# A key-value product with high and low halves side by side, and denominators in another order

## The chip, the cores and the metric

The kernel runs on one core of one Trainium2 chip. The core has five engines with an instruction stream each: TensorE (PE in the profile, with its weight loads shown apart as PEld), VectorE (DVE), ScalarE (ACT), GpSimd (POOL) and SyncE (SP, which here only issues DMAs). They meet through semaphores. The metric is the device time of one launch in microseconds, the median of several runs.

## The reference

The reference is one transformer block on a prompt of 2048 tokens of width 512, modulated by a condition vector. Cut to what matters here:

```
h = layernorm(x) * (1 + ca) + sa
q, k, v = split(h @ wqkv) into 32 heads of 16
pq, pk = phi(q), phi(k)          # phi(t) = (t + 1 if t > 0 else exp(t)) + 1e-6
kv  = sum over tokens of pk^T v  # a 16 x 16 block for each head
z   = sum over tokens of pk
o   = (pq kv) / (pq z + 1e-6)
x   = x + ga * (o @ wo)
...                              # then a second norm and a gated feed-forward block
```

All of it is float32.

## The kernel before, in words

The tokens are four chunks of 512, each chunk four tiles of 128 tokens, sixteen tiles in all; numbers 0 to 15 below are these. A matmul takes 128 x 128 weights and a moving operand of up to 512 columns. To keep float32 accuracy, each operand is split into a high part (a copy rounded to the format that TensorE takes, made by ScalarE) and a low part (the rest, a subtraction on VectorE), and a product is three matmuls: high by high, high by low, low by high. The function `product` (lines 215 to 221) issues these three for each of the four 128-row pieces of the contraction; `split` (lines 205 to 207) makes the two parts.

The kernel never forms the value vectors of all tokens. It sums over the tokens the product of the normed input and the key features, a 512 x 512 matrix T (in four PSUM banks, `tacc`), and gets the key-value blocks from T and the value weights afterwards. This is the small product of the change: `kv_part` (lines 789 to 796). For each of four pieces k of the contraction and each of four groups g of 128 output columns it issues the three matmuls with 128 moving columns: 48 in all, into one PSUM bank. Before it, `tt_high` (lines 780 to 784) adds the shift to a piece of T and has ScalarE copy out the high part, and `tt_low` (line 787) subtracts for the low part. After it, one VectorE multiplication (line 818) keeps the 16 x 16 blocks on the diagonal and clears the rest, and the result is split and multiplied by the output weights: `w_full` makes the folded weight of one group (product, then a multiplication by the gate at line 770), `w_split` its two parts.

The query features of a tile come from `proj` (a product), `q_a` (two ScalarE instructions, lines 327 and 328) and `q_b` (one on VectorE, line 331). The denominators are computed tile by tile: `den_p` multiplies the features by z (line 712, on POOL unless VectorE is named), `den_r` sums 16 neighbours (line 718, VectorE), `den_z` makes a constant that all tiles share (lines 706 and 707), `den_b` adds it and takes the reciprocal for a whole chunk at once (lines 727 and 728), `den_t` does the reduction, the addition and the reciprocal for single tiles (lines 734 to 736), and `den_c` divides the features (line 747). `den_q` is `den_p` on POOL for tiles by their running number.

The order of work is written out by hand: each engine runs its instructions in the order in which the program issues them, and a wait holds up what stands behind it on that engine. The part around the change stands in lines 774 to 835, and behind it come sixteen steps `y_step(i)`. In step i TensorE turns the features of tile i + 1 (`turn_a`, four transposes, line 846), which needs their division by `den_c(i + 1)`, and then forms the output of tile i (`y_a`, line 871), which needs the high part (ScalarE, line 850) and the low part (VectorE, line 854) of the turned tile i. In the lists of `after` stand further jobs: denominators, the sums of weight blocks of the feed-forward part (`right_sums`, four subtractions on POOL at line 1002) and their splits (`right_split`, low parts on POOL at line 1020).

SBUF tiles come from one pool of 99 buffers; PSUM has four banks for sums (`acc`) and four for products that are read at once (`bank`).

Of the kernel before, what the change touches and what calls it, by code (L numbers as in the profile page):

```python
# [9 lines left out]
F32R = mybir.dt.float32r  # L10
# [12 lines left out]
def tile_adaln_block(  # L23
# [41 lines left out]
    def f32(ap):  # L65
        return ap.bitcast(F32)
# [138 lines left out]
    def split(src, h, l, low=None):  # L205
        nc.scalar.activation(h, src, AF.Copy)  # L206
        (low or nc.vector).tensor_tensor(l, src, f32(h), op=ALU.subtract)  # L207
# [27 lines left out]
    def cut(pair, a, b):  # L235
        return pair[0][:, a:b], pair[1][:, a:b]
# [409 lines left out]
    for i in range(4, NT):  # L646
        ch, j = divmod(i, NJ)
        more = ch + 1 < NCH
        if i > 1:
            ahead[i + 2] = proj(i + 2, wk) if i + 2 < NT else proj(i + 6 - NT, wq)  # L650
        if i in q_at:
            qps = proj(q_at[i], wq)
        if i + 1 < NT:
            k_split_x(i + 1)
        if i + 1 < NT:
            k_split(i + 1)
        if more and j < 2:
            t_tile(i, 0, 1)
            nx.transpose(2 * j, 2 * j + 1)
            nx.modulated(ca, sa, 2 * j, 2 * j + 1, cast=nc.vector)  # L660
            norm[ch + 1:] = [nx]
        if ch + 2 < NCH and j == 1:
            nx2 = Norm(xts[ch + 2])
            nx2.stats(0, 1)
        if ch + 2 < NCH and j == 2:
            nx2.stats(2, 3)
            nx2.rstd_of()
        if ch + 2 < NCH and j == 3:
            nx = nx2
            nx.xhat(2)  # L670
        if i + 2 < NT:
            k_phi(i + 2, ahead.pop(i + 2))
        else:
            q_a(i + 6 - NT, ahead.pop(i + 2))
            q_b(i + 6 - NT)
        if i in q_at:
            q_a(q_at[i], qps)
            q_b(q_at[i])
        if i + 1 < NT:
            z_add(i + 1)  # L680
        if i + 1 == NT - 1:
# [12 lines left out]
        if i in extra:  # L694
            extra[i]()
    ga, gb, sb, cb = rows[2], rows[5], cols[3], cols[4]


# [5 lines left out]
    def den_z():  # L704

        nc.vector.reduce_sum(den0, zb.rearrange("p (h i) -> p h i", i=DH), axis=AX.X)
        nc.vector.tensor_scalar(den0, den0, EPS_PHI, EPS_DEN, op0=ALU.mult, op1=ALU.add)

    def den_p(ch, *js, on=None):
        for j in js:  # L710
            pzs[ch, j] = B("f")
            (on or nc.gpsimd).tensor_tensor(pzs[ch, j], phq[ch * NJ + j], zb, op=ALU.mult)  # L712

    def den_r(ch, *js):
        if ch not in dens:
            dens[ch] = T(small, "den", (P, NJ, NH))
        for j in js:
            nc.vector.reduce_sum(dens[ch][:, j], pzs.pop((ch, j)).rearrange("p (h i) -> p h i", i=DH), axis=AX.X)

    def den_a(ch, *js, on=None):  # L720

        for j in js:
            den_p(ch, j, on=on)
            den_r(ch, j)

    def den_b(ch):
        nc.vector.tensor_tensor(dens[ch], dens[ch], den0.unsqueeze(1).to_broadcast([P, NJ, NH]), op=ALU.add)
        nc.vector.reciprocal(dens[ch], dens[ch])

    def den_t(*tiles):  # L730
        for i in tiles:
            ch, j = divmod(i, NJ)
            den_r(ch, j)
            d = dens[ch][:, j]
            nc.vector.tensor_tensor(d, d, den0, op=ALU.add)
            nc.vector.reciprocal(d, d)

    def den_q(*tiles):
        for i in tiles:
# [31 lines left out]
            fs.append(f)  # L771
        return fs

    den_z()
    den_p(1, 0, 1)
    den_a(0, 0, 1, on=nc.vector)
    ps = proj(6, wq)
    fs, tt = [], []

    def tt_high(k):  # L780
        f = fs[k]
        nc.vector.scalar_tensor_tensor(f, zb, sa[:, k:k + 1], f, op0=ALU.mult, op1=ALU.add)
        tt.append((B("w", dt=F32R), B("w", dt=F32R)))
        nc.scalar.activation(tt[k][0], f, AF.Copy)

    def tt_low(k):
        nc.vector.tensor_tensor(tt[k][1], fs[k], f32(tt[k][0]), op=ALU.subtract)
# [20 lines left out]
    kvps = acc_bank()  # L808
# [7 lines left out]
    kvp = (B("xh", dt=F32R), B("xl", dt=F32R))  # L816
    kvf = B("n")
    nc.vector.tensor_tensor(kvf.rearrange("p (g c) -> p g c", g=KD), kvps.rearrange("p (g c) -> p g c", g=KD),
                            mask.unsqueeze(1).to_broadcast([P, KD, P]), op=ALU.mult)
    split(kvf, *kvp)  # L820
    q_a(8, ps)
    ps = proj(9, wq)
    q_b(8)
    den_b(0)
    q_a(9, ps)
    w_out(0, 1)
# [514 lines left out]
    y_step(4, q=12, after=[lambda: n2[0].rstd_of(3, 4, True), lambda: n2[0].xhat(0, 1, 2), lambda: den_t(8), lambda: den_q(10, 11)])  # L1341
    y_step(5, pre=[lambda: n2[0].xhat(3)], after=[lambda: den_t(9), lambda: den_q(12), lambda: right_sums(1)])
    y_step(6, pe=[lambda: ln2_turn(0, 0, 1)], after=[lambda: ln2_f(0, 0, 1), lambda: den_t(10), lambda: right_split(1)])
    for k in range(KH):
        lefts[k] = Left((0, 1), k).into(side)
    right_load(2)
    reload_x(12, 13, 14, 15)
    y_step(7, q=13, pe=[lambda: ln2_turn(0, 2, 3)], after=[lambda: n2[1].rstd_of(0, 3, True), lambda: ln2_f(0, 2, 3), lambda: den_t(11), lambda: L[0].split("a11")])
    y_step(8, after=[lambda: n2[1].rstd_of(3, 4, True), lambda: den_q(13), lambda: n2[1].xhat(0, 1, 2), lambda: den_t(12), lambda: L[1].split("a11")])
    y_step(9, q=14, pre=[lambda: n2[1].xhat(3)], pe=[lambda: ln2_turn(1, 0, 2)], mid=[lambda: ln2_f(1, 0, 2)],  # L1350
           after=[lambda: L[0].sum("s1"), lambda: den_t(13), lambda: L[0].split("a12"), lambda: L[0].sum("s3", on=nc.gpsimd)])
# [252 lines left out]
```

## Time and profile before

| | |
|---|---|
| time, median of 3 runs | 554.49 us (553.54 to 554.92) |
| span of the profiled execution | 552.4 us |
| TensorE busy | 545.8 us, 99% of the span |
| VectorE busy | 432.2 us, 78% |
| ScalarE busy | 299.5 us, 54% |
| GpSimd busy | 176.8 us, 32% |
| mean granted TensorE clock | 0.999 |

The page gives the span of the profiled execution, from its first to its last instruction; a run's time holds what lies around the span too. In a timeline, each row is one instruction or a run of equal ones: start, length, engine, line of the kernel, operation, output and inputs, shapes, count, and in brackets how long the engine stood idle before it and what ended that. A row of TensorE shows a matmul with its drain, so that rows overlap; what a matmul costs in a stream is the distance between starts. On VectorE, starts in a row of 512-column instructions are some 0.6 us apart, although each row is 0.68 long. A row that is longer than others of its shape has stood and waited in itself.

### The profile page before, as it was taken

The page shows a single profiled execution, that of the slowest core. Times are in us where ns is not written, and L with a number is a line of the kernel's source. Part 1 is how long each engine was busy: PE and PEld are TensorE (multiplying, and loading weights), DVE is VectorE, ACT ScalarE, POOL GpSimd, SP SyncE. Part 2 cuts the span into 40 slices and gives each one's busy share as a digit, 9 for nine tenths or more (in the row PEclk, how much of TensorE's full clock was granted, in tenths as well). Part 3 has the DMA queues.
Part 4 walks back from the last instruction along what each step waited for, and adds up shares of the span by engine and source line. Part 5 has one row for each costly group of instructions (what it writes and reads, how often), then busy time and mean ns, then how long its engine had stood idle before and what let it go on. Part 6 is the DMA issues. An engine that isn't in the chain of part 4 may idle for free. (4 is left out here: it accounts for less than half of the span.)

```text
span 552.4 us, 8146 instructions
## 1 busy us (share of the span) xinstructions
PE 545.8 (99%) x2775; PEld 460.1 (83%) x2775; DVE 432.2 (78%) x794; ACT 299.5 (54%) x535; POOL 176.8 (32%) x180
## 2 busy tenths in 40 slices
PE   8999999999999999999999999999999999999997
PEld 6888888888888888888888888878888888888886
DVE  6878779978998998865655767797577877879696
ACT  4876857456467876654545355463243534453540
POOL 2000000003527646353556644540002524242400
PEclk9999999999999999999999999999999999999999
DMA  8910224203230045195888634289786534342004
GB/s 256 373 57 1 76 77 152 77 0 77 78 115 2 0 154 189 39 316 180 285 286 274 222 123 163 87 312 391 231 259 218 173 131 138 129 146 86 1 0 153
DMA packets 58512, 83.24 MB, mean 151 GB/s; under 512 B 6564, under 2 KB 23720, under 8 KB 58472
## 3 DMA queue, kind: packets, MB, share of 16 engines
q1 hardware_dynamic: 56544, 81.16, 44.1%
q10 hardware_dynamic: 1928, 1.58, 0.9%
q8 instruction: 22, 0.36, 0.3%
q14 instruction: 18, 0.15, 0.1%
HBM read 53.02 MB, written 29.69 MB: 150 GB/s over the span
## 5 line engine op out<-in xcount | busy, mean ns | idle before, releaser
L1057 PE MATMUL bank<-h,w 128*128 128x512 f32 (+1 forms) x924 | 221.6, 391 | 0.2 <-POOL w L1020 0.2
L1057 PEld LDWEIGHTS bank<-h,w 128*128 128x128 f32 (+1 forms) x924 | 168.2, 186 | 36.2 <-POOL w L1020 0.6
L1063 ACT ACTIVATE bank<-bank 128x512 f32<-128x512 f32 (+2 forms) x46 | 26.2, 571 | 122.7 <-PE bank L1057 122.5
L1253 DVE TENSOR_TENSOR x<-acc,x 128x256 f32<-128x256 f32 x132 | 48.0, 414 | 13.7 <-PE acc L1226 13.1
L1226 PE MATMUL acc<-w,kh 128*128 128x256 f32 x308 | 57.1, 282 | 0.0
L1226 PEld LDWEIGHTS acc<-w,kh 128*128 128x128 f32 x308 | 50.6, 190 | 3.7
L1020 POOL TENSOR_TENSOR w<-raw,w 128x256 fp32r<-128x256 f32 (+3 forms) x22 | 24.7, 1121 | 73.7 <-ACT w L1013 64.1
L219 PE MATMUL bank<-w,h 128*128 128x512 f32 x112 | 44.1, 394 | 0.0
L221 PE MATMUL bank<-w,h 128*128 128x512 f32 x112 | 43.7, 390 | 0.0
L220 PE MATMUL bank<-w,h 128*128 128x512 f32 x112 | 43.6, 390 | 0.0
L1226 PE MATMUL acc<-w,kl 128*128 128x256 f32 x154 | 43.5, 283 | 0.0
L871 PE MATMUL acc<-w,xh 128*128 128x512 f32 x128 | 40.7, 399 | 0.0
L712 POOL TENSOR_TENSOR f<-h,zb 128x512 f32<-128x512 f32 x12 | 17.5, 1468 | 62.9 <-ACT zb L692 48.9
L262 POOL TENSOR_TENSOR rstd<-ve,half 128x4 f32<-128x4 f32 (+3 forms) x12 | 11.2, 935 | 81.4 <-DVE ve L259 68.0
L1083 DVE TENSOR_TENSOR phi<-bank,g 128x512 f32<-128x512 f32 (+1 forms) x22 | 15.1, 687 | 25.2 <-PE bank L1057 25.2
L1063 ACT ACTIVATE u<-bank 128x512 f32<-128x512 f32 (+1 forms) x44 | 26.1, 594 | 15.4 <-PE bank L1057 15.2
L1113 DVE TENSOR_TENSOR g<-bank,u 128x512 f32<-128x512 f32 (+1 forms) x22 | 15.2, 689 | 21.2 <-ACT u L1063 19.9
L1020 POOL TENSOR_TENSOR w<-t,w 128x512 fp32r<-128x512 f32 (+1 forms) x22 | 29.6, 1346 | 0.0
L1146 PE MATMUL acc<-w,kh 128*128 128x512 f32 (+1 forms) x76 | 29.6, 390 | 0.0
L1147 PE MATMUL acc<-w,kh 128*128 128x512 f32 (+1 forms) x76 | 29.6, 390 | 0.0
L1148 PE MATMUL acc<-w,kl 128*128 128x512 f32 (+1 forms) x76 | 29.6, 389 | 0.0
L277 ACT ACTIVATE n<-x,nmr,rstd 128x512 f32<-128x512 f32 x31 | 23.6, 808 | 10.9 <-DVE nmr L267 10.7
(204 smaller groups left out, 1187.0 us busy)
## 6 DMA issues: line engine op xcount, KB each, us to landing
right<-w SPq DMA_DIRECT2D x56, 256.0 KB, 3.7
w<-right SPq DMA_DIRECT2D x56, 256.0 KB, 4.3
x<-in_A_x_dram SPq DMA_DIRECT2D x22, 256.0 KB, 5.2
raw<-in_w_mod_dram SPq DMA_DIRECT2D x22, 256.0 KB, 3.7
raw<-in_B_w_down_dram SPq DMA_DIRECT2D x18, 256.0 KB, 3.0
side_s<-h SPq DMA_DIRECT2D x16, 256.0 KB, 2.6
h<-side_s SPq DMA_DIRECT2D x16, 256.0 KB, 5.3
raw<-in_A_wqkv_dram SPq DMA_DIRECT2D x12, 256.0 KB, 6.2
```

Source lines behind the costliest of these rows:

```text
L219: nc.tensor.matmul(ps, ah, bh, start=begin and i == 0, stop=False)
L220: nc.tensor.matmul(ps, ah, bl, start=False, stop=False)
L221: nc.tensor.matmul(ps, al, bh, start=False, stop=end and i == n - 1)
L871: nc.tensor.matmul(yps[i], x, y, start=fresh and k + n == 0, stop=k == KD - 1 and n == 2, skip_group_check=True)
L1020: sub = lambda out, x, y: (on or nc.gpsimd).tensor_tensor(out, x, f32(y), op=ALU.subtract)
L1057: mm = lambda x, y, **kw: nc.tensor.matmul(ps, x[:, k], y, skip_group_check=True, **kw)
L1063: nc.scalar.activation(out, x, AF.Copy)
L1146: nc.tensor.matmul(dn[j], hh[:n, a:b], dh[:n], start=i == 0, stop=False)
L1147: nc.tensor.matmul(dn[j], hh[:n, a:b], dl[:n], start=False, stop=False)
L1148: nc.tensor.matmul(dn[j], hl[:n, a:b], dh[:n], start=False, stop=i == n_of - 1)
L1226: mm = lambda x, y, **kw: nc.tensor.matmul(ps, x[:, a:b], y, skip_group_check=True, **kw)
L1253: nc.vector.tensor_tensor(xt[:, halves[at]], banks[b][m], xt[:, halves[at]], op=ALU.add)
```

## The change

Three things change.

First, the high and the low part of T lie side by side. For each piece k of the contraction and each half s of the columns there is a tile that holds, for each of two groups, 128 high and then 128 low columns. One matmul of 256 columns takes the high weights past both, and a second of 128 columns takes the low weights past the high columns: 32 matmuls in place of 48. The sums of high by low now stand apart, in the second 128 columns of each group, in two PSUM banks. They are copied to SBUF by ScalarE (`kv_side`) and added by two products with the identity (`kv_join`), which stand in the middle of the projection of tile 9. The mask is applied half by half (`kv_mask`). The identity is copied once into TensorE's format, in the key loop at tile 12. The splits of T become two instructions of 256 columns each in place of one of 512.

Second, of the multiplications of chunk 0 POOL takes tiles 2 and 3, and VectorE tiles 0 and 1, one of them ahead of the work on T and one behind it. The shared constant moves behind the query features of tiles 6 and 7. POOL takes tiles 6 and 4 after those features, and 8, 5 and 7 after the features of tile 8; before it had 4 and 5 first, then 6 and 7, and 8 in step 1.

Third, `den_t` takes two tiles in one addition and one reciprocal; the reductions stay single. Steps 0, 2, 4, 6 and 9 each handle a pair where single tiles were handled in almost every step.

```diff
@@ key loop
+        if i == NT - 4:
+            ident_r = B("w", (P, P), F32R)
+            nc.scalar.activation(ident_r, ident, AF.Copy)
@@ den_t
         for i in tiles:
-            ch, j = divmod(i, NJ)
-            den_r(ch, j)
-            d = dens[ch][:, j]
-            nc.vector.tensor_tensor(d, d, den0, op=ALU.add)
-            nc.vector.reciprocal(d, d)
+            den_r(*divmod(i, NJ))
+        (ch, a), n = divmod(tiles[0], NJ), len(tiles)
+        d = dens[ch][:, a:a + n]
+        nc.vector.tensor_tensor(d, d, den0.unsqueeze(1).to_broadcast([P, n, NH]), op=ALU.add)
+        nc.vector.reciprocal(d, d)
@@ around the small product
-    den_z()
-    den_p(1, 0, 1)
-    den_a(0, 0, 1, on=nc.vector)
+    den_p(0, 2, 3)
+    den_a(0, 0, on=nc.vector)
     ps = proj(6, wq)
...
-        tt.append((B("w", dt=F32R), B("w", dt=F32R)))
-        nc.scalar.activation(tt[k][0], f, AF.Copy)
+        tt.append([B("w", (P, KG, 2, P), F32R) for _ in range(2)])
+        for s in range(2):
+            nc.scalar.activation(tt[k][s][:, :, 0], pairs_of(f)[:, s], AF.Copy)
...
-        nc.vector.tensor_tensor(tt[k][1], fs[k], f32(tt[k][0]), op=ALU.subtract)
+        for s in range(2):
+            nc.vector.tensor_tensor(tt[k][s][:, :, 1], pairs_of(fs[k])[:, s], f32(tt[k][s])[:, :, 0], op=ALU.subtract)
...
-            for g in range(KD):
-                a, b = g * P, (g + 1) * P
-                (ah, al), (bh, bl) = cut(wv[k], a, b), cut(tt[k], a, b)
-                for n, (x, y) in enumerate(((ah, bh), (ah, bl), (al, bh))):
-                    nc.tensor.matmul(kvps[:, a:b], x, y, start=k + g + n == 0, stop=k == KD - 1 and n == 2,
+            for s in range(2):
+                for g in range(KG):
+                    a = (s * KG + g) * P
+                    (ah, al), both_b = cut(wv[k], a, a + P), tt[k][s][:, g]
+                    nc.tensor.matmul(kvps[s][:, g], ah, both_b, start=k + g == 0, stop=False, skip_group_check=True)
+                    nc.tensor.matmul(kvps[s][:, g, 0], al, both_b[:, 0], start=False, stop=k == KD - 1,
...
+    def kv_side(s):
+        kv_more.append(B("xh", (P, KG, P), F32R))
+        nc.scalar.activation(kv_more[s], kvps[s][:, :, 1], AF.Copy)
+    def kv_join(s):
+        nc.tensor.matmul(kvps[s][:, :, 0], ident_r, kv_more[s], start=False, stop=True, skip_group_check=True)
+    def kv_mask(s):
+        nc.vector.tensor_tensor(kvf[:, s], kvps[s][:, :, 0], mask.unsqueeze(1).to_broadcast([P, KG, P]), op=ALU.mult)
...
+    den_a(0, 1, on=nc.vector)
     q_a(6, ps)
...
-    den_p(1, 2)
+    den_p(1, 2, 0)
     ps = proj(8, wq)
-    den_a(0, 2, 3, on=nc.vector)
+    den_z()
+    den_r(0, 2, 3)
     kv_part(2, 3)
...
+    kv_side(0)
+    kv_side(1)
     q_a(8, ps)
-    ps = proj(9, wq)
+    ps = bank()
+    pairs = [(cut(norm[2].t[k], P, 2 * P), wq[k]) for k in range(KD)]
+    product(ps, pairs[:2], end=False)
+    kv_join(0)
+    kv_join(1)
+    product(ps, pairs[2:], begin=False)
+    kv_mask(0)
+    kv_mask(1)
+    split(kvf.rearrange("p s g c -> p (s g c)"), *kvp)
     q_b(8)
+    den_p(2, 0)
+    den_p(1, 1, 3)
     den_b(0)
@@ output steps
-    y_step(0, after=[lambda: q_b(11), lambda: den_q(7), lambda: den_t(4), lambda: right_sums(0)])
-    y_step(1, after=[lambda: den_t(5), lambda: den_q(8)])
-    y_step(2, after=[lambda: den_t(6), lambda: den_q(9), lambda: right_split(0)])
-    y_step(3, after=[lambda: den_t(7), lambda: n2[0].rstd_of(0, 3, True)])
+    y_step(0, after=[lambda: q_b(11), lambda: den_t(4, 5), lambda: right_sums(0)])
+    y_step(1, after=[lambda: den_q(9)])
+    y_step(2, after=[lambda: den_t(6, 7), lambda: right_split(0)])
+    y_step(3, after=[lambda: n2[0].rstd_of(0, 3, True)])
...
```

The steps from 4 on change in the same way: pairs (8, 9), (10, 11) and (12, 13) in steps 4, 6 and 9; tiles 14 and 15 stay single.

More of the change, by code (lines that the diff above doesn't have):

```diff
@@ L772, in w_full, with pairs_of @@
         return fs
-    den_z()
-    den_p(1, 0, 1)
-    den_a(0, 0, 1, on=nc.vector)
+    den_p(0, 2, 3)
+    den_a(0, 0, on=nc.vector)
     ps = proj(6, wq)
     fs, tt = [], []
+    KG = KD // 2
+    def pairs_of(x):
+        return x.rearrange("p (s g c) -> p s g c", s=2, g=KG)
     def tt_high(k):
@@ L782, in tt_high @@
         nc.vector.scalar_tensor_tensor(f, zb, sa[:, k:k + 1], f, op0=ALU.mult, op1=ALU.add)
-        tt.append((B("w", dt=F32R), B("w", dt=F32R)))
-        nc.scalar.activation(tt[k][0], f, AF.Copy)
+        tt.append([B("w", (P, KG, 2, P), F32R) for _ in range(2)])
+        for s in range(2):
+            nc.scalar.activation(tt[k][s][:, :, 0], pairs_of(f)[:, s], AF.Copy)
     def tt_low(k):
-        nc.vector.tensor_tensor(tt[k][1], fs[k], f32(tt[k][0]), op=ALU.subtract)
+        for s in range(2):
+            nc.vector.tensor_tensor(tt[k][s][:, :, 1], pairs_of(fs[k])[:, s], f32(tt[k][s])[:, :, 0], op=ALU.subtract)
     def kv_part(*ks):
         for k in ks:
-            for g in range(KD):
-                a, b = g * P, (g + 1) * P
-                (ah, al), (bh, bl) = cut(wv[k], a, b), cut(tt[k], a, b)
-                for n, (x, y) in enumerate(((ah, bh), (ah, bl), (al, bh))):
-                    nc.tensor.matmul(kvps[:, a:b], x, y, start=k + g + n == 0, stop=k == KD - 1 and n == 2,
-                                     skip_group_check=True)
+            for s in range(2):
[4 more added lines that the diff above has]
+                    nc.tensor.matmul(kvps[s][:, g, 0], al, both_b[:, 0], start=False, stop=k == KD - 1,
+                                     skip_group_check=True)
+    kv_more = []
+    def kv_side(s):
[3 more added lines that the diff above has]
+        nc.tensor.matmul(kvps[s][:, :, 0], ident_r, kv_more[s], start=False, stop=True, skip_group_check=True)
+    kvf = B("n", (P, 2, KG, P))
+    kvp = (B("xh", (P, D), F32R), B("xl", (P, D), F32R))
+    def kv_mask(s):
+        nc.vector.tensor_tensor(kvf[:, s], kvps[s][:, :, 0], mask.unsqueeze(1).to_broadcast([P, KG, P]), op=ALU.mult)
     for k in range(KD):
@@ L805, in tile_adaln_block @@
     tt_low(KD - 1)
+    den_a(0, 1, on=nc.vector)
     q_a(6, ps)
     q_tile(7)
-    kvps = acc_bank()
+    kvps = [T(ps_acc, "acc", (P, KG, 2, P)) for _ in range(2)]
     kv_part(0, 1)
@@ L811, in tile_adaln_block @@
     q_b(7)
-    den_p(1, 2)
+    den_p(1, 2, 0)
     ps = proj(8, wq)
-    den_a(0, 2, 3, on=nc.vector)
+    den_z()
+    den_r(0, 2, 3)
     kv_part(2, 3)
[L816 to L820, printed above, removed]
-    q_a(8, ps)
-    ps = proj(9, wq)
+    kv_side(0)
+    kv_side(1)
+    q_a(8, ps)
+    ps = bank()
[7 more added lines that the diff above has]
+    split(kvf.rearrange("p s g c -> p (s g c)"), *kvp)
     q_b(8)
+    den_p(2, 0)
+    den_p(1, 1, 3)
     den_b(0)
@@ L1335, in tile_adaln_block @@
     right_load(1)
-    y_step(0, after=[lambda: q_b(11), lambda: den_q(7), lambda: den_t(4), lambda: right_sums(0)])
-    y_step(1, after=[lambda: den_t(5), lambda: den_q(8)])
-    y_step(2, after=[lambda: den_t(6), lambda: den_q(9), lambda: right_split(0)])
-    y_step(3, after=[lambda: den_t(7), lambda: n2[0].rstd_of(0, 3, True)])
+    y_step(0, after=[lambda: q_b(11), lambda: den_t(4, 5), lambda: right_sums(0)])
+    y_step(1, after=[lambda: den_q(9)])
+    y_step(2, after=[lambda: den_t(6, 7), lambda: right_split(0)])
+    y_step(3, after=[lambda: n2[0].rstd_of(0, 3, True)])
     reload_x(8, 9, 10, 11)
-    y_step(4, q=12, after=[lambda: n2[0].rstd_of(3, 4, True), lambda: n2[0].xhat(0, 1, 2), lambda: den_t(8), lambda: den_q(10, 11)])
-    y_step(5, pre=[lambda: n2[0].xhat(3)], after=[lambda: den_t(9), lambda: den_q(12), lambda: right_sums(1)])
-    y_step(6, pe=[lambda: ln2_turn(0, 0, 1)], after=[lambda: ln2_f(0, 0, 1), lambda: den_t(10), lambda: right_split(1)])
+    y_step(4, q=12, after=[lambda: n2[0].rstd_of(3, 4, True), lambda: n2[0].xhat(0, 1, 2), lambda: den_t(8, 9), lambda: den_q(10, 11)])
+    y_step(5, pre=[lambda: n2[0].xhat(3)], after=[lambda: den_q(12), lambda: right_sums(1)])
+    y_step(6, pe=[lambda: ln2_turn(0, 0, 1)], after=[lambda: ln2_f(0, 0, 1), lambda: den_t(10, 11), lambda: right_split(1)])
     for k in range(KH):
@@ L1347, in tile_adaln_block @@
     reload_x(12, 13, 14, 15)
-    y_step(7, q=13, pe=[lambda: ln2_turn(0, 2, 3)], after=[lambda: n2[1].rstd_of(0, 3, True), lambda: ln2_f(0, 2, 3), lambda: den_t(11), lambda: L[0].split("a11")])
-    y_step(8, after=[lambda: n2[1].rstd_of(3, 4, True), lambda: den_q(13), lambda: n2[1].xhat(0, 1, 2), lambda: den_t(12), lambda: L[1].split("a11")])
+    y_step(7, q=13, pe=[lambda: ln2_turn(0, 2, 3)], after=[lambda: n2[1].rstd_of(0, 3, True), lambda: ln2_f(0, 2, 3), lambda: L[0].split("a11")])
+    y_step(8, after=[lambda: n2[1].rstd_of(3, 4, True), lambda: den_q(13), lambda: n2[1].xhat(0, 1, 2), lambda: L[1].split("a11")])
     y_step(9, q=14, pre=[lambda: n2[1].xhat(3)], pe=[lambda: ln2_turn(1, 0, 2)], mid=[lambda: ln2_f(1, 0, 2)],
-           after=[lambda: L[0].sum("s1"), lambda: den_t(13), lambda: L[0].split("a12"), lambda: L[0].sum("s3", on=nc.gpsimd)])
+           after=[lambda: L[0].sum("s1"), lambda: den_t(12, 13), lambda: L[0].split("a12"), lambda: L[0].sum("s3", on=nc.gpsimd)])
     y_step(10, pe=[lambda: ln2_turn(1, 1, 3)], mid=[lambda: ln2_f(1, 1, 3)],
```

## The prediction

> **What bounds the kernel now.** I read the page's busy shares first, then TensorE's own waits (between 120 and 340 us that answer is empty), then the table by stretches and the timelines of the engines around the edit. The shares, and three stretches (in each row the columns are the stretch, its length, and the busy time of PE, PEld, DVE, ACT and POOL with instruction counts, then PE clock and DMA):
>
> ```profile
> span 552.4 us, 8146 instructions
> ## 1 busy us (share of the span) xinstructions
> PE 545.8 (99%) x2775; PEld 460.1 (83%) x2775; DVE 432.2 (78%) x794; ACT 299.5 (54%) x535; POOL 176.8 (32%) x180
> ```
> ```profile
> 132.94:135.57 2.63, 2.63 (x26) 2.63 (x24) 2.53 (x5) 1.90 (x4) 0.00 (x0) 1.00 0.80 201
> 138.40:141.03 2.63, 2.63 (x26) 2.63 (x24) 2.56 (x4) 0.00 (x0) 2.63 (x2) 1.00 0.00 0
> 143.00:156.00 13.00, 13.00 (x63) 10.62 (x62) 12.52 (x21) 8.76 (x16) 3.19 (x3) 1.00 0.22 70
> ```
>
> TensorE is never idle here, so each microsecond taken from it is worth one, and each wait put in front of it costs one. The third row holds the danger: behind the small product DVE works 12.52 of 13.00 us. It is no bound there, but it has 0.48 us to spare, while POOL works only 3.19 us. TensorE's timeline behind the small product, the dates that the other engines must meet:
>
> ```profile
> 143.86 0.39 PE L219 MATMUL bank<-w,xh 128*128 128x512 f32 x1
> ...
> 150.67 0.60 PE L846 MATMUL bank<-ident,h 128*128 128x128 f32 x4
> ...
> 152.97 0.73 PE L871 MATMUL acc<-w,xh 128*128 128x512 f32 x2
> 153.53 0.40 PE L871 MATMUL acc<-w,xl 128*128 128x512 f32 x1
> ...
> 159.06 0.60 PE L846 MATMUL bank<-ident,h 128*128 128x128 f32 x4
> ```
>
> 143.86 is the first use of the masked product, 150.67 the turn of query tile 0, 152.97 the first output product and 153.53 its third matmul (the first that needs a low part), 159.06 the turn of tile 3.
>
> **The change, part by part.** *The product on TensorE.* Each half of it, 24 matmuls of 128 columns, took 2.63 us: 0.110 each. A half now has 8 of 256 columns and 8 of 128. For 256 columns with new weights each time, the chain of work has:
>
> ```profile
> 412.66 1.43 PE acc L1226 x12
> ```
>
> That is 0.119 each, so a half costs 8 x 0.119 + 8 x 0.110 = 1.83 and saves 0.80; both save 1.60. The two identity products have 256 columns: 0.24. Net -1.36. Bounds: a wide matmul costs no less than a narrow one (net -1.51) and no more than two narrow ones (net +0.24). I take 0.119, the same shape. A rule bears on this: the Trainium skill, "TensorE: Matmul & The Clock Gate", section Back-to-back issue gap, gives some 81 ns for each 128-column matmul that brings its own weights. By that figure the 16 matmuls saved would be worth 1.3 us instead of 1.75, and the whole forecast would rise by about 0.45 (an estimate from that page). The trace's 110 ns does not agree and decides.
>
> *The splits of T.* Four ACT copies and four DVE subtractions become eight each, of half the width. Before, the last two subtractions were:
>
> ```profile
> 134.15 1.47 DVE L787 TENSOR_TENSOR w<-n,w 128x512 fp32r<-128x512 f32 x2
> 141.95 0.63 ACT L206 ACTIVATE xh<-n 128x512 fp32r<-128x512 f32 x1 [4.75 <-DVE n L818]
> L1253 DVE TENSOR_TENSOR x<-acc,x x132: 405/414/425, 370.7 to 541.2; 128x256 f32<-128x256 f32 x132
> ```
>
> They ended at 135.62. The second half of the product now starts at 138.40 - 0.80 = 137.60, so 2 us cover them, and DVE also starts on T earlier, as the shared denominator and one of its two early tiles move behind it. I price the split at nothing; without the cover it would be four times 2 x 0.41 - 0.68, 0.6 us. The copy of the identity is one small ACT instruction long before its use: nothing. DVE loses two multiplications of chunk 0 to POOL and gets one back later; by 141.2 its queue is empty enough for the mask.
>
> *The join.* The second half ends at 141.03 - 1.60 = 139.43. Two ACT copies must be done when the six matmuls put between (half of 143.86 - 141.03, 1.42) are through, at 140.85. The first bank closes four matmuls early, so even at the 0.63 of a full-width copy they end near 140.4. The joins end at 141.1. Two masks of 0.41 (the L1253 row) follow, started a little apart: 141.95. The high copy, 0.63: 142.6. The low part, 0.68 with POOL out of the way: 143.35. TensorE has finished the other six matmuls at 142.5, waits 0.2 for the high part, and 0.25 before its third matmul for the low. Of 1.36 some 0.9 is left: it leaves this place 0.9 early.
>
> *The denominators.* Here I expect the gain to go. DVE and POOL as they were:
>
> ```profile
> 142.62 1.19 DVE L207 TENSOR_TENSOR xl<-n,xh 128x512 fp32r<-128x512 f32 x1 [0.70 <-ACT xh L206]
> 143.77 0.69 DVE L331 SCALAR_TENSOR_TENSOR h<-bank,h 128x512 f32<-128x512 f32 x1
> ...
> 146.89 1.29 DVE L207 TENSOR_TENSOR w<-n,w 128x512 fp32r<-128x512 f32 x2
> 148.10 0.68 DVE L331 SCALAR_TENSOR_TENSOR h<-bank,h 128x512 f32<-128x512 f32 x1
> 148.70 0.68 DVE L747 SCALAR_TENSOR_TENSOR h<-h,den 128x512 f32<-128x512 f32 x1
> 149.30 1.28 DVE L770 TENSOR_TENSOR n<-bank,row 128x512 f32<-128x512 f32 x2
> 150.50 0.68 DVE L747 SCALAR_TENSOR_TENSOR h<-h,den 128x512 f32<-128x512 f32 x1
> 151.10 0.68 DVE L207 TENSOR_TENSOR w<-n,w 128x512 fp32r<-128x512 f32 x1
> 151.94 0.69 DVE L854 TENSOR_TENSOR xl<-bank,xh 128x512 fp32r<-128x512 f32 x1 [0.15 <-ACT xh L850]
> 152.54 0.68 DVE L207 TENSOR_TENSOR w<-n,w 128x512 fp32r<-128x512 f32 x1
> ...
> 155.82 0.68 DVE L718 TENSOR_REDUCE den<-f 128x32 f32<-128x512 f32 x1
> 156.53 0.19 DVE L735 TENSOR_TENSOR den<-den,den 128x32 f32<-128x32 f32 x1
> 156.75 0.35 DVE L736 RECIPROCAL den<-den 128x32 f32<-128x32 f32 x1
> 157.02 0.63 DVE L747 SCALAR_TENSOR_TENSOR h<-h,den 128x512 f32<-128x512 f32 x1
> ```
> ```profile
> 142.52 0.74 POOL L1002 TENSOR_TENSOR t<-raw,t 128x256 f32<-128x256 f32 x1
> 144.60 1.31 POOL L712 TENSOR_TENSOR f<-h,zb 128x512 f32<-128x512 f32 x1 [1.34 <-PE bank L220]
> 148.93 1.62 POOL L712 TENSOR_TENSOR f<-h,zb 128x512 f32<-128x512 f32 x1 [3.02 <-DVE h L331]
> ```
>
> A DVE instruction that reads two SBUF tiles and a POOL instruction do not run together: the subtraction at 142.62 took 1.19 for its usual 0.68, until POOL's instruction of 142.52 had ended and 0.55 more. Where both have a queue they take turns:
>
> ```profile
> 217.46 0.74 POOL L1002 TENSOR_TENSOR t<-raw,t 128x256 f32<-128x256 f32 x1
> 218.16 1.19 POOL L1002 TENSOR_TENSOR t<-raw,raw 128x256 f32<-128x256 f32 x1
> ```
> ```profile
> 217.53 2.36 DVE L207 TENSOR_TENSOR h<-s,h 128x512 fp32r<-128x512 f32 x2
> ```
>
> Two subtractions took 2.36 there and 1.29 at 146.89. The Trainium skill, "SBUF — State Buffer", section Who interferes with whom, calls it an exclusive lock for a whole instruction and exempts DVE instructions with one SBUF input; if the four of those in this stretch waited too, 0.5 us each as at 142.62, my sum would rise by 2 us (an estimate).
>
> POOL's order is now: tiles 2 and 3 of chunk 0, then 6 and 4, then 8, 5 and 7, then the four weight sums of the first right block (0.74 each, before done by 143.26), then 9. Tile 8 needs the query feature that DVE finishes behind the mask and the split, at about 144.0, so POOL stands idle until then and after it works without a pause: three multiplications of some 1.25, four sums, one more multiplication, 8 us of work from 144.15, where 2.9 us stood. On DVE it meets six two-tile instructions. DVE arrives 0.5 early (no 1.19 this time). Asked, granted, ended:
> - low of output weight 0: asked 146.39, POOL's second multiplication ends 146.63, done 147.2 (before 147.57).
> - low of weight 1: behind POOL's third, 148.45; done 149.0 (before 148.18).
> - division of query tile 0: asked 149.54, behind the first sum; done 150.3 (before 149.38).
> - division of tile 1: asked 151.43, behind the third; done 152.3 (before 151.18).
> - low of weight 2: behind the fourth sum; done 153.6 (before 151.78). Then the low of the turned tile 0, which waits for nobody: 154.25 (before 152.63).
> - low of weight 3: behind the multiplication of tile 9; done 155.4 (before 153.22).
>
> 3.5 us of waits. The pair of denominators adds a reduction (0.71 with its gap) and some 0.2 of reciprocal ahead of the division of tile 3: 160.5 where it was 157.65. The pairs save six additions and the start of six reciprocals later, some 1.5 us of DVE, on which TensorE does not wait.
>
> Against TensorE's dates: tile 0 turns at 150.36 (wanted 149.8 with the 0.9 in hand; before 150.67). The third matmul of the first output product waits for 154.25 plus a signal: 154.3, against 153.53, +0.77. The turn of tile 3 waits for the division at 160.5: 160.56, against 159.06, +1.5. Behind it DVE has caught up: its next pair comes only after two steps, and tile 5's turn lies behind a whole query projection. Each of the six waits is good to 0.3; bounds of their sum are 0 (POOL always loses) and 6 us (each meets a POOL instruction at its start). I take +1.4.
>
> **The sum.** The profiled execution spans 552.4, the median is 554.49, so 2.1 lies around the span and stays. 552.4 + 1.4 + 2.1 = 555.9.
>
> **Rivals.** *Slower by more.* The first of the six waits has a margin of 0.24: if POOL's second multiplication ends before 146.39 instead of at 146.63, the low of weight 0 waits for the whole third one, the low of weight 1 then ends at 149.5, and 0.5 more is carried to tile 3: 556.4 and, where the sums fall badly too, up to 557.4. For it: the margin is smaller than my error. Against: POOL's start at 144.15 follows DVE's own work, so both shift together. Chance 0.30.
> *The gain stays.* DVE had finished the division of tile 0 at 149.38 for a turn at 150.67, 1.3 early; if POOL gives way more often than the rows at 217 show, that slack covers the lateness: 554.49 - 0.9 = 553.6. Chance 0.20.
> *No gain at all.* The 256 columns cost as much as two narrow matmuls: the product saves nothing, everything behind comes 1.6 later: 557.5. Against: the L1226 row. Chance 0.04.
> The forecast has 0.46.
>
> **How the numbers follow.** About 0.3%, 1.66 us, is what a measurement of this kernel can tell from no change. The gain rival reaches 552.8 with a quarter of its chance: faster 0.05. The forecast lies within, with 0.06 of its 0.46 beyond 556.15: same 0.40 + 0.15 = 0.55; slower 0.06 + 0.30 + 0.04 = 0.40. The range runs from a little under the gain rival, 553.4, to the bad end of the slower one, 557.4.
>
> **What would show it.** Right: the small product at 0.114 per matmul; POOL unbroken from 144 to 155; lows at L207 and divisions at L747 of 1.2 to 1.9 us there; PE waits named after DVE at the first output product and the turn of tile 3. Wrong: those lows at 0.68, PE without a gap until 170, or POOL done with the sums before 144.

## The result, and the profile after

The kernel after takes 557.05 us (median of 5 runs, 556.37 to 557.51), the kernel before 554.49 us (5 runs, 553.54 to 555.01): a ratio of 1.0044, 95% interval 1.0032 to 1.0056. It is slower by 2.56 us. The profiled execution spans 555.0 us where 552.4 stood. From the page (busy us of each engine, its share of the span, its instructions), and the table by stretches with the two halves of the small product and the 13 us behind it (columns as in the prediction):

```profile
span 555.0 us, 8120 instructions
PE 545.8 (98%) x2761; PEld 458.8 (83%) x2761; DVE 428.3 (77%) x787; ACT 300.5 (54%) x542; POOL 180.6 (33%) x182
```
```profile
132.80:134.59 1.79, 1.79 (x17) 1.79 (x16) 1.79 (x6) 1.18 (x4) 0.00 (x0) 1.00 0.24 60
137.40:139.19 1.79, 1.79 (x17) 1.79 (x16) 1.75 (x4) 0.26 (x1) 1.79 (x2) 1.00 0.85 239
143.00:156.00 13.00, 12.11 (x56) 9.40 (x56) 12.86 (x19) 7.51 (x14) 10.10 (x8) 1.00 0.19 65
```

Each half of the product went from 2.63 to 1.79 us. In the third row POOL went from 3.19 to 10.10 us, and TensorE, which had no gap there, stands still for 0.89 us. VectorE has fewer instructions in that row (19 for 21) and is busier: the longer ones stand and wait inside themselves. TensorE's own waits between 120 and 340 us (what it waited for, then us in total, times, longest), where the answer of before was empty:

```profile
PE bank L881 <- DVE h L750: 1.4, 2, 1.2
PE bank L219 <- DVE h L331: 0.9, 1, 0.9
```

The answer counts from the end of a matmul's row, drain included (148.04 + 0.39 to 149.32 is 0.89). So it shows a stop shorter than it is in the stream of starts, and leaves short ones out: 142.42 stands 0.40 behind 142.02 instead of the usual 0.23. TensorE's timeline around these waits:

```profile
142.02 0.40 PE L221 MATMUL bank<-w,h 128*128 128x512 f32 x1
142.42 0.50 PE L219 MATMUL bank<-w,xh 128*128 128x512 f32 x1
142.76 0.40 PE L220 MATMUL bank<-w,xh 128*128 128x512 f32 x1
143.15 0.50 PE L221 MATMUL bank<-w,xl 128*128 128x512 f32 x1
143.49 0.39 PE L219 MATMUL bank<-w,xh 128*128 128x512 f32 x1
...
148.04 0.39 PE L221 MATMUL bank<-w,xl 128*128 128x512 f32 x1
149.32 0.50 PE L219 MATMUL bank<-w,h 128*128 128x512 f32 x1 [0.89 <-DVE h L331]
...
150.82 0.60 PE L881 MATMUL bank<-ident,h 128*128 128x128 f32 x4
...
153.69 0.40 PE L906 MATMUL acc<-w,xl 128*128 128x512 f32 x1
...
159.60 0.66 PE L881 MATMUL bank<-ident,h 128*128 128x128 f32 x4 [0.26 <-DVE h L750]
...
174.98 0.39 PE L906 MATMUL acc<-w,xl 128*128 128x512 f32 x1
176.55 0.63 PE L881 MATMUL bank<-ident,h 128*128 128x128 f32 x4 [1.19 <-DVE h L750]
```

Against the same places of before, TensorE uses the masked product at 142.42 (before 143.86, -1.44), turns tile 0 at 150.82 (150.67, +0.15), reaches the third matmul of the first output product at 153.69 (153.53, +0.16), turns tile 3 at 159.60 (159.06, +0.54) and tile 7 at 176.55 (174.72, +1.83). The last turn, of tile 15, stays +1.82 late (239.69 for 237.87) and TensorE's last matmul +1.85 (550.08 for 548.23). Of the 1.44, 0.14 was there before the product began (132.80 for 132.94). So three places make the loss: the wait at 149.32, which eats the whole gain of the product (from 1.03 early at 148.04 to 0.15 late), tile 3, which adds some 0.4, and tile 7, which adds 1.2. VectorE's and POOL's timelines of after at these places:

```profile
146.13 2.54 DVE L207 TENSOR_TENSOR w<-n,w 128x512 fp32r<-128x512 f32 x2
148.59 0.68 DVE L331 SCALAR_TENSOR_TENSOR h<-bank,h 128x512 f32<-128x512 f32 x1
149.19 0.68 DVE L750 SCALAR_TENSOR_TENSOR h<-h,den 128x512 f32<-128x512 f32 x1
149.79 1.28 DVE L773 TENSOR_TENSOR n<-bank,row 128x512 f32<-128x512 f32 x2
150.99 0.73 DVE L750 SCALAR_TENSOR_TENSOR h<-h,den 128x512 f32<-128x512 f32 x1
151.63 1.22 DVE L207 TENSOR_TENSOR w<-n,w 128x512 fp32r<-128x512 f32 x1
...
153.38 1.19 DVE L207 TENSOR_TENSOR w<-n,w 128x512 fp32r<-128x512 f32 x1
...
158.92 0.63 DVE L750 SCALAR_TENSOR_TENSOR h<-h,den 128x512 f32<-128x512 f32 x1
...
172.44 1.27 DVE L721 TENSOR_REDUCE den<-f 128x32 f32<-128x512 f32 x2
173.74 0.95 DVE L738 TENSOR_TENSOR den<-den,den 128x64 f32<-128x64 f32 x1
174.73 0.55 DVE L739 RECIPROCAL den<-den 128x64 f32<-128x64 f32 x1
175.20 1.21 DVE L750 SCALAR_TENSOR_TENSOR h<-h,den 128x512 f32<-128x512 f32 x1
```
```profile
143.84 4.27 POOL L715 TENSOR_TENSOR f<-h,zb 128x512 f32<-128x512 f32 x3 [4.37 <-DVE h L331]
148.08 1.17 POOL L1037 TENSOR_TENSOR t<-raw 128x256 f32<-128x256 f32 x1
149.32 1.14 POOL L1037 TENSOR_TENSOR t<-raw,t 128x256 f32<-128x256 f32 x1
...
152.27 1.75 POOL L715 TENSOR_TENSOR f<-h,zb 128x512 f32<-128x512 f32 x1
...
173.31 4.24 POOL L715 TENSOR_TENSOR f<-h,zb 128x512 f32<-128x512 f32 x3
```

*At 149.32.* The first product of the projection of tile 11 needs a PSUM bank, and that bank holds the projection of tile 9 until `q_b(9)`, the L331 row at 148.59, has read it. That row stands behind the two subtractions of 146.13, which took 2.54 us in place of 1.29, since POOL's block of three multiplications runs beside them. Before, `q_b(9)` ended at 148.10 + 0.68 = 148.78 for a matmul at 149.30: a margin of 0.52. Now it ends 0.49 later (149.27), and TensorE comes 1.03 earlier: 0.49 + 1.03 - 0.52 = 1.00 too late, and the gap in the stream is 149.32 - 148.04 - 0.23 = 1.05.

*At tile 3.* Before, the division ended at 157.02 + 0.63 = 157.65, 1.41 ahead of the turn at 159.06. Now it ends at 159.55: the last low part of the output weights ends 1.35 later (154.57 for 153.22), and the pair (4, 5) puts a second reduction and a longer reciprocal ahead of the division. Neither alone uses up the 1.41.

*At tile 7.* Before, VectorE and TensorE did this (their timelines, the same place):

```profile
172.53 0.19 DVE L735 TENSOR_TENSOR den<-den,den 128x32 f32<-128x32 f32 x1
...
173.03 1.54 DVE L747 SCALAR_TENSOR_TENSOR h<-h,den 128x512 f32<-128x512 f32 x1
```
```profile
174.36 0.39 PE L871 MATMUL acc<-w,xl 128*128 128x512 f32 x1
174.72 0.63 PE L846 MATMUL bank<-ident,h 128*128 128x128 f32 x4
```

There one instruction, the division, stood behind a multiplication of POOL, and ended at 174.57. The turn began 0.36 behind the matmul before it, not 0.23: this date had no margin left, though no wait is listed there. With the pair (8, 9) a second reduction comes first, and the addition then starts behind POOL's first multiplication (0.95 instead of 0.19) and the division behind its second: it ends at 176.41, and the turn begins 1.57 behind the matmul before it.

Beyond the +1.85 at TensorE's last matmul, the two spans differ by another 0.71: from that matmul to the end there were 4.17 us before and 4.88 after. The kernels below have 4.66 to 5.21 there, the fastest of them too, so I don't put this to the change; it stays open.

### The profile page after: what moved, and what is told of

Its sections match the earlier page's. It is cut to its first block, busy times and chain, and to the rows that moved or that the text cites. A ratio compares the mean times of both kernels' runs of the same rounds, so it can differ in the third digit from the quotient of the medians.

```text
span 555.0 us, 8120 instructions
## 1 busy us (share of the span) xinstructions
PE 545.8 (98%) x2761; PEld 458.8 (83%) x2761; DVE 428.3 (77%) x787; ACT 300.5 (54%) x542; POOL 180.6 (33%) x182
## 5 line engine op out<-in xcount | busy, mean ns | idle before, releaser
L715 POOL TENSOR_TENSOR f<-h,zb 128x512 f32<-128x512 f32 x14 | 20.2, 1457 | 63.1 <-ACT zb L692 48.8
L1261 PEld LDWEIGHTS acc<-w,kl 128*128 128x128 f32 x154 | 29.4, 191 | 0.0
```

The lines of the kernel that those rows point to most:

```text
L1261: mm = lambda x, y, **kw: nc.tensor.matmul(ps, x[:, a:b], y, skip_group_check=True, **kw)
```

## The experiments

All compute the whole result. "At the product" is the start of the product's first matmul against the kernel before (132.94), "at tile 15" that of the last turn (237.87), and "between" their difference. The first differs from one profiled execution to the next by more than these edits explain: e8 is the same program as the kernel before up to step 0 and yet 0.40 late there, e3 the same as the change and 0.34 later. So it is "between" that tells of an edit.

| run | median us (before beside it) | ratio, 95% interval | TensorE at the product | at tile 15 | between |
|---|---|---|---|---|---|
| the change | 557.05 (554.49) | 1.0044, 1.0032 to 1.0056 | -0.14 | +1.82 | +1.96 |
| e1_product | 554.45 (554.53) | 1.0002, 0.9986 to 1.0019 | -0.14 | -0.27 | -0.13 |
| e2_dens | 556.83 (554.53) | 1.0051, 1.0037 to 1.0065 | -0.17 | +2.30 | +2.47 |
| e3_singles | 555.34 (554.53) | 1.0014, 1.0005 to 1.0023 | +0.20 | +0.70 | +0.50 |
| e4_ahead | 555.90 (554.53) | 1.0039, 1.0022 to 1.0057 | -0.18 | +0.96 | +1.14 |
| e5_both | 554.70 (554.32) | 1.0009, 1.0001 to 1.0018 | -0.18 | -0.24 | -0.06 |
| e6_bank | 557.39 (554.32) | 1.0071, 1.0049 to 1.0093 | -0.06 | +2.57 | +2.63 |
| e7_sums_last | 553.73 (554.32) | 0.9993, 0.9984 to 1.0001 | -0.25 | -1.00 | -0.75 |
| e8_pairs | 555.26 (554.32) | 1.0019, 1.0010 to 1.0027 | +0.40 | +1.59 | +1.19 |
| e9_best | 553.42 (554.52) | 0.9983, 0.9972 to 0.9993 | -0.15 | -1.60 | -1.45 |

The differences of the medians lie up to 0.6 us from "between", so a part of that size can't be read from them.

My theory after the result: two causes add up, POOL's unbroken block behind the product (which delays `q_b(9)`) and the pairs (which delay tile 7). The rivals: the new product itself costs something, through the joins and their copies; or one date alone, the bank, is at fault.

**e1_product: the product alone.** The kernel before with the new product and joins; all denominators as before.

```diff
 # against the kernel after
-    den_p(0, 2, 3)
-    den_a(0, 0, on=nc.vector)
+    den_z()
+    den_p(1, 0, 1)
+    den_a(0, 0, 1, on=nc.vector)
...
-    den_p(2, 0)
-    den_p(1, 1, 3)
...
```

> The new product and join, with every denominator where it was before the change. Theory (the product gains, the denominators lose it): TensorE reaches the first use of the masked product about 1.4 us earlier; POOL's weight sums stand at 140 to 143 us again, so the low part of the masked product (142.4) takes 1.2 us instead of 0.7 and costs TensorE some 0.5 at its third matmul; after that no wait. 553.6 to 554.0, that is 0.5 to 0.9 under the kernel before. Rival (the product with its copies and joins is itself what costs): 555 or more.

It is as fast as before, so the time missed both the theory (553.6 to 554.0) and the rival. TensorE uses the masked product 1.32 early and keeps 0.27, or 0.13 counted from the product. Its one wait, and what VectorE and POOL did there:

```profile
PE bank L221 <- DVE xl L207: 0.6, 1, 0.6
```
```profile
142.52 1.27 DVE L207 TENSOR_TENSOR xl<-n,xh 128x512 fp32r<-128x512 f32 x1 [0.70 <-ACT xh L206]
```
```profile
142.51 0.74 POOL L1034 TENSOR_TENSOR t<-raw,t 128x256 f32<-128x256 f32 x1
```

The subtraction for the masked product's low part starts 0.01 us behind POOL's last weight sum and waits for all of it. The product brings something, and POOL takes most of that back at once, by an instruction that the change did not touch.

**e2_dens: the denominators alone.** The old product with the new order of denominators and the pairs.

```diff
 # against the kernel before
-    den_z()
-    den_p(1, 0, 1)
-    den_a(0, 0, 1, on=nc.vector)
+    den_p(0, 2, 3)
+    den_a(0, 0, on=nc.vector)
...
+    den_p(2, 0)
+    den_p(1, 1, 3)
...
-    y_step(0, after=[lambda: q_b(11), lambda: den_q(7), lambda: den_t(4), lambda: right_sums(0)])
+    y_step(0, after=[lambda: q_b(11), lambda: den_t(4, 5), lambda: right_sums(0)])
...
```

> The old product with the denominators of the changed kernel. Theory: the wait for the bank of tile 9 (1.05 us in the changed kernel, with TensorE 1.0 early) is about nothing, since TensorE comes at its old date 149.3; the wait at the turn of tile 3 (about 0.5) and the one at the turn of tile 7 (about 1.2) stay: 556.0 to 556.6. Rival (the product costs): 554.5.

The denominators alone cost 2.30 us, slightly more than I had expected. The waits:

```profile
PE bank L849 <- DVE h L747: 1.5, 2, 1.2
PE bank L219 <- DVE h L331: 0.5, 1, 0.5
```

I had expected no wait for the bank without the product's gain; there is one of 0.5. So `q_b(9)` is late by itself, and the product's gain only makes TensorE earlier for it.

**e3_singles: the change without the pairs.**

```diff
-    y_step(0, after=[lambda: q_b(11), lambda: den_t(4, 5), lambda: right_sums(0)])
-    y_step(1, after=[lambda: den_q(9)])
+    y_step(0, after=[lambda: q_b(11), lambda: den_t(4), lambda: right_sums(0)])
+    y_step(1, after=[lambda: den_t(5), lambda: den_q(9)])
...
```

> The changed kernel with its pairs undone: each denominator finished alone, at the step where it was before; POOL's new order stays. Theory with two causes (POOL's block behind the product, and the pairs): the bank's wait of 1.05 stays, the waits at the turns of tiles 3 and 7 (0.4 and 1.2) go: 1.5 to 1.7 under the changed kernel, 555.3 to 555.6. Rival with one cause (all the lateness comes from POOL's block): the same time as the changed kernel, 557.

TensorE gets back 1.96 - 0.50 = 1.46 us, the time 1.71. The wait for the bank stays at 0.9, the one at tile 3 goes, the one at tile 7 falls to 0.2.

**e8_pairs: the pairs alone.** The kernel before, with `den_t` and the steps as in the kernel after.

```diff
 # against the kernel before
-    y_step(2, after=[lambda: den_t(6), lambda: den_q(9), lambda: right_split(0)])
-    y_step(3, after=[lambda: den_t(7), lambda: n2[0].rstd_of(0, 3, True)])
+    y_step(2, after=[lambda: den_t(6, 7), lambda: den_q(9), lambda: right_split(0)])
+    y_step(3, after=[lambda: n2[0].rstd_of(0, 3, True)])
...
```

> The kernel before with nothing but the pairs. Theory with two causes: the pairs alone make TensorE wait at the turn of tile 7 (1.2 us, where the addition and the division each stand behind one of POOL's multiplications of tiles 10 and 11), and nothing at tile 3, for which VectorE was 1.4 early: 555.5 to 555.9. Rival (POOL's block is the only cause; fewer instructions on VectorE help): 554.5 or less.

The wait at tile 7 is there with nothing else changed (TensorE's waits, and VectorE's timeline):

```profile
PE bank L846 <- DVE h L747: 1.2, 1, 1.2
```
```profile
173.51 0.96 DVE L735 TENSOR_TENSOR den<-den,den 128x64 f32<-128x64 f32 x1
...
174.97 1.21 DVE L747 SCALAR_TENSOR_TENSOR h<-h,den 128x512 f32<-128x512 f32 x1
```

TensorE is 0.39 late ahead of tile 7, all of it from ahead of the product, where nothing was changed, and 1.59 behind it: 1.2 us are the pair's. At tile 3 nothing is lost. The time, 0.94 above the kernel before, is a little under what I had expected, and excludes the rival.

**e4_ahead: POOL's jobs earlier.** The change, with tiles 5 and 7 multiplied ahead of the query features of tile 8 instead of behind them.

```diff
-    den_p(1, 2, 0)
+    den_p(1, 2, 0, 1, 3)
...
     den_p(2, 0)
-    den_p(1, 1, 3)
```

> The changed kernel with POOL's multiplications of tiles 5 and 7 moved ahead of that of tile 8, into the 4.4 us in which POOL stood idle. Theory with two causes: the bank's wait shrinks from 1.05 to 0.3 or less and that at the turn of tile 3 goes, that at the turn of tile 7 stays near 1.2, since VectorE waits for TensorE just before it (1.7 us idle at 170): 555.3 to 555.8. Rival with one cause (POOL's block alone): all three waits go, 553.6 or less. Rival (pairs alone): 557.

TensorE gets back 1.96 - 1.14 = 0.82; the bank's wait falls from 0.9 to 0.5, not to nothing, and the time ends just above the range. The wait at tile 3 goes here too; the one at tile 7 stays at 1.2, against the rival with POOL's block alone. The two subtractions still take turns, now with POOL's sums of 0.74 instead of multiplications of 1.25 (VectorE's timeline):

```profile
146.09 2.16 DVE L207 TENSOR_TENSOR w<-n,w 128x512 fp32r<-128x512 f32 x2
```

**e5_both: e3 and e4 together.**

```diff
-    den_p(1, 2, 0)
+    den_p(1, 2, 0, 1, 3)
...
-    y_step(0, after=[lambda: q_b(11), lambda: den_t(4, 5), lambda: right_sums(0)])
+    y_step(0, after=[lambda: q_b(11), lambda: den_t(4), lambda: right_sums(0)])
...
```

> The changed kernel with both moves of the two runs before it: tiles 5 and 7 ahead on POOL, and the denominators finished singly. Theory with two causes, adding up: TensorE 0.25 early after the bank's wait, as with the move alone, and 0.2 to 0.3 lost at the turn of tile 7, as with the singles alone: 554.2 to 554.8, the time of the kernel before. Rival (the two hide one another): 555 or more.

The two together give back nearly everything: -0.06 is left between product and tile 15, and the bank's 0.5 is the only wait. They add up but for one place: 1.96 - 1.46 - 0.82 would be -0.32. The wait at tile 3 went with either edit, and stands in no kernel that has only one of the causes (e3, e4, e8) but in e2, which has both; so it needs both, and the sum counts it twice. The time is as expected, but 0.38 above the kernel before, with an interval just clear of 1.

**e6_bank: the bank freed first.** The change, with `q_b(9)` ahead of the two subtractions that delayed it.

```diff
-    w_out(0, 1)
+    wf = w_full(0, 1)
     q_b(9)
+    for f in wf:
+        w_split(f)
```

> The changed kernel with the query features of tile 9 finished before the two splits of the output weights, so that their bank comes free 2.4 us earlier; POOL's block and the pairs stay. Theory (POOL's turns make VectorE late, and the bank was only the first date it missed): the bank's wait goes, but TensorE meets VectorE 0.3 us later at the turn of tile 0 and some 0.7 at the third matmul of the first output product; the waits at tiles 3 and 7 stay: 556.3 to 557.0. Rival (the bank's order is the cause): 1.0 under the changed kernel, 556.0 or less.

It is slower than I expected. TensorE is also later than in the change (+2.63 for +1.96); in the times, 1.0071 and 1.0044, the intervals overlap. TensorE's waits, and VectorE's timeline:

```profile
PE bank L883 <- DVE n L773: 1.4, 1, 1.4
PE bank L883 <- DVE h L750: 1.2, 1, 1.2
PE acc L908 <- DVE xl L891: 0.5, 1, 0.5
```
```profile
146.02 0.68 DVE L331 SCALAR_TENSOR_TENSOR h<-bank,h 128x512 f32<-128x512 f32 x1
146.62 2.81 DVE L207 TENSOR_TENSOR w<-n,w 128x512 fp32r<-128x512 f32 x2
149.36 1.22 DVE L750 SCALAR_TENSOR_TENSOR h<-h,den 128x512 f32<-128x512 f32 x1
150.50 1.28 DVE L773 TENSOR_TENSOR n<-bank,row 128x512 f32<-128x512 f32 x2
```

The bank of tile 9 is free in time. The next bank is not: tile 0's turn waits 1.4 us for the one that the gate's multiplication (L773) frees, and the first output product then waits for a low part, as I had predicted for the change. So the rival of one date falls. VectorE's queue as a whole is late, and reordering it moves the wait to another date.

**e7_sums_last: the product, with the weight sums out of the way.** As e1, but POOL multiplies tiles 4 to 9 first and takes the weight sums of the right block last.

```diff
 # against e1_product
-    den_p(1, 2)
+    den_p(1, 2, 3)
...
     q_b(8)
+    den_p(2, 0)
...
     q_b(9)
+    den_p(2, 1)
...
-    y_step(0, after=[lambda: q_b(11), lambda: den_q(7), lambda: den_t(4), lambda: right_sums(0)])
+    y_step(0, after=[lambda: q_b(11), lambda: den_t(4), lambda: right_sums(0)])
...
```

> The new product with the single denominators, and POOL's four weight sums moved behind the multiplications of tiles 7, 8 and 9, away from the low part of the masked product (which cost the product alone 0.6 at TensorE) and from the splits of the first two output weights. Theory: the low part takes 0.7, TensorE keeps 1.0 of its lead, the sums stand at 150 to 153 us where VectorE has more than 1 us in hand: 553.4 to 553.8. Rival (the turn-taking moves with the sums): 554.5.

TensorE has no wait listed and keeps 1.00, or 0.75 counted from the product. The time is at the edge of what can be told. Run again, beside e9:

> The kernel with the sums moved last, again, beside the one above and on the same chip: 553.4 to 553.9, TensorE 1.0 early from 150 us on.

That gave 554.36 us against 554.52, ratio 1.0002 (0.9981 to 1.0022): e7 isn't told apart from before, though TensorE has no wait listed in its first profile. The second profile is 2.19 late at the product, ahead of the change's place; from there to tile 15 it gains 0.76, as the first did (0.75).

**e9_best: the change with its causes taken out.** Single denominators; tiles 5 and 7 early; tile 9 ahead of the weight sums, as in e7; and the joins one quarter earlier in the projection of tile 9.

```diff
 # against the kernel after
-    den_p(1, 2, 0)
+    den_p(1, 2, 0, 1, 3)
...
-    product(ps, pairs[:2], end=False)
+    product(ps, pairs[:1], end=False)
     kv_join(0)
     kv_join(1)
-    product(ps, pairs[2:], begin=False)
+    product(ps, pairs[1:], begin=False)
...
     den_p(2, 0)
-    den_p(1, 1, 3)
...
     q_b(9)
+    den_p(2, 1)
...
-    y_step(0, after=[lambda: q_b(11), lambda: den_t(4, 5), lambda: right_sums(0)])
-    y_step(1, after=[lambda: den_q(9)])
+    y_step(0, after=[lambda: q_b(11), lambda: den_t(4), lambda: right_sums(0)])
+    y_step(1, after=[lambda: den_t(5)])
...
```

> Everything learned in one kernel: the new product, chunk 0's multiplications as in the change (two tiles on POOL), single denominators, POOL's tiles 5 and 7 ahead of 8 and its weight sums behind 9, and the two joins after three matmuls of the projection of tile 9 instead of six. Theory: VectorE stood idle 1.5 us before the masks, so the masks start 0.7 earlier, TensorE no longer waits for the masked product's parts (0.4), and keeps 1.3 to 1.4 of its lead: 553.0 to 553.5. Rival (the fourth multiplication on POOL, to 142.0, now meets the low part): 553.7, no better than the sums moved last.

It is faster than both kernels: 553.42 us (11 runs, 552.63 to 553.90) against 554.52 for the one before beside it, with an interval just clear of 1. It was not measured a second time, as e7 was. TensorE has no wait listed between 120 and 340 us. From the table by stretches, and VectorE's timeline:

```profile
143.00:156.00 13.00, 13.00 (x64) 10.68 (x63) 12.79 (x23) 8.62 (x17) 7.68 (x6) 1.00 0.19 62
```
```profile
140.25 0.76 DVE L822 TENSOR_TENSOR n<-acc,mask 128x256 f32<-128x256 f32 x2 [0.81 <-PE acc L816]
...
145.56 1.29 DVE L207 TENSOR_TENSOR w<-n,w 128x512 fp32r<-128x512 f32 x2
146.78 0.68 DVE L331 SCALAR_TENSOR_TENSOR h<-bank,h 128x512 f32<-128x512 f32 x1
```

POOL still works 7.68 us of the 13, but not beside the two subtractions: they take 1.29 again, and `q_b(9)` ends at 147.46 instead of 149.27. The earlier joins start VectorE's chain 0.7 us sooner (140.25 for 140.95). Which of the four edits brings how much wasn't tried one by one.

## Why the prediction was right or wrong

The sign and the kind of loss were right: the product gains, the denominators lose more. The sum, +1.4, was too small: +2.56 in the medians, +1.82 located on TensorE. That it came so near is in part luck: up to tile 3, all that the prediction priced, TensorE was 0.54 late instead of 1.5, and tile 7, which it put at nothing, cost 1.2. Step by step:

- **The product: right.** 1.79 us a half against 1.83, so the two halves and the joins give 2 x 0.84 - 0.24 = 1.44, against 1.36. The Trainium skill, "TensorE: Matmul & The Clock Gate", section Back-to-back issue gap, would have 81 ns for a 128-column matmul with its own weights. The 24 of a half before took 110 ns each, and the 16 here, half of them 256 columns wide, 112; the row was the better guide.
- **The splits at nothing: right.** Both halves begin without a gap, 0.23 behind the matmul before them (132.57 to 132.80, 137.17 to 137.40).
- **The join: right.** TensorE was to leave this place 0.9 early; at 148.04 it was 1.03 early, of which 0.14 was there before the product.
- **POOL's unbroken block: right.** 143.84 to 154.02, predicted from 144.15.
- **The turns of VectorE and POOL: right where it counted, too large in sum.** The low of weight 1 was to end at 149.0 and ended at 148.67. The two divisions, which were to wait for the sums, hardly did: 0.68 and 0.73 us. The first started at 149.19, as POOL's first sum came to its end (149.25), and it was POOL's second sum that waited (1.14). The lengthenings are 2.54 - 1.29, 0.05, 0.54 and 0.51, together 2.35 instead of 3.5. (The 3.5 is more than the prediction's own rows give: the last low 2.18 later than before, after a start 0.5 earlier, is 2.68. The forecast goes by the dates and doesn't use it.) The other term that the prediction kept apart, four VectorE instructions with one SBUF input, cost nothing: L331 took 0.68 and L773 1.28 for two, as before. There the section Who interferes with whom of the Trainium skill's page "SBUF — State Buffer", which exempts them, and the trace agree.
- **TensorE's dates: wrong place.** I listed tile 0's turn, the first low part and tile 3's turn. The date that was missed isn't among them: the release of a PSUM bank by `q_b(9)`. Its margin before, 0.52, could have been read from the rows that the prediction quotes (L331 at 148.10) and TensorE's next projection at 149.30. Once TensorE had lost its lead there, the first two of my dates were met with nothing further lost (+0.15, +0.16), and tile 3 cost 0.38 where I had 0.73 (from +0.77 to +1.5).
- **"Behind it DVE has caught up" and the pairs "on which TensorE does not wait": this step failed.** I priced six additions and six reciprocals saved, and looked for what the first pair delays, but not at the later ones. The pair (8, 9) stands ahead of tile 7's division, brings a reduction of some 0.6 us that wasn't there (1.27 for two), and so pushes two of VectorE's instructions behind POOL's multiplications: 1.2 us, shown alone by e8 and down to 0.2 in e3.
- **The rivals.** "Slower by more" gave the right region by a mechanism that didn't happen: the low of weight 0 didn't wait for the whole third multiplication, or the pair of lows would have ended at 149.5. "The gain stays" and "No gain at all" are excluded by the waits and by the 1.79.

## What to carry to other kernels

Before a second engine's jobs are moved into a stretch where the first one is busy 12.5 of 13 us, list every date that the first engine must meet there, the release of each PSUM bank among them, with its margin: the smallest margin limits what any gain ahead of it can be worth, and repairing one missed date (e6) only shows the next. A pair of small jobs is done no earlier than its later member: the instructions it saves count for less than what it puts ahead of the first user, above all where the other engine shares the reads. Once a change has lost, its parts can be run alone: here e9 keeps the product and part of POOL's new order, without the pairs and without POOL's unbroken block.

## What the runs showed of the hardware that I had not expected

After a wait, TensorE's next matmul of 512 columns starts 0.34 us after the first instead of 0.23: 142.42 to 142.76, 143.15 to 143.49, and 149.32 to 149.66. Each stop so costs some 0.11 us more than its gap: at 149.32 the gap was 1.05, and a lead of 1.03 had become a lag of 0.15 by the turn of tile 0. A wait is not the only thing that brings the longer step: in the kernel before, 0.32 stands behind the four transposes of 150.67 without one (151.02 to 151.34).

A small VectorE instruction waits for POOL as a large one does: the addition of 128 x 64 elements took 0.95 and 0.96 us at tile 7 (after and e8), and 0.23 at 158.19 in the kernel after, where POOL stands idle. The kernel before had shown it too (its 128 x 32 additions took 0.19 at 172.53 and 1.27 at 181.05), and I had not looked there.
